# Batch 1's attention issued earlier on TensorE, weight splitting released sooner and paced, and a second PSUM bank for h

## The chip, the cores and the metric

The kernel runs on one core of one Trainium2 chip. Times are device microseconds (us) of one launch; lower is better. Engines are called as the profile calls them: PE is TensorE's matmuls and PEld its weight loads, DVE is VectorE, ACT is ScalarE, POOL is GpSimd, SP is SyncE, whose queue issues every DMA here.

## The reference

```python
def reference(q, k, v, phi, moe_w_in, moe_w_out, moe2_w_in, moe2_w_out):
    # q, k, v: 4 batches x 8 heads x 576 tokens x 64; phi: 4 x 8 x 576 x 32 slots
    a = softmax(phi, axis=2)                     # over the tokens
    k_m, v_m = a^T k, a^T v                      # 32 x 64 per head
    attn = softmax(q k_m^T / 8)                  # 576 x 32 per head
    x = (attn v_m)  -> 2304 tokens x 512
    y = relu(x w_in)^2 w_out                     # 512 -> 2048 -> 512
    h = y w_in2;  g = h tanh(softplus(h))
    return g w_out2                              # 512 -> 2048 -> 512
```

All of it is float32. Each matmul of the two MLPs is done as three products of a high and a low part (high x high, high x low, low x high), so every weight is split into such parts on the chip, too.

## The kernel before

The first MLP is the stage of this change. It works on tiles of half a batch (288 tokens), named by batch and half: `10` is batch 1, half 0. A tile goes through 16 steps `fc`, one for each 128 columns of the hidden layer. A step on PE is six matmuls into one bank (`h10_3` is step 3 of tile 10; L464 to L466), then on ACT a Relu (L472), a Square (L473) and a cast to the high part (L477), on DVE a subtraction that leaves the low part (L480), and three steps later (`LAG`) twelve matmuls of the second weight, `mm2_step`, into four accumulators (L428 to L430; their operand is `g10_3`).

Weights for h are not `w_in` itself: attention's last product (with `v_m`) is folded into it, so `w_part` multiplies the value memory `vT` of a batch with a page of `w_in` (`pw120` is batch 1, page 2; one page serves two steps), and ACT and DVE split the result (`wp`).

Batches 0 and 1 are worked through together, because the first weights arrive while they run: `subs` lists twelve passes, three groups of steps (0 to 3, 4 to 9, 10 to 15) times four tiles (00, 01, 10, 11). In the text, pass 2 is tile 10 of the first group, and so on from pass 0 to pass 11. Batches 2 and 3 follow in passes of 16 steps: pass 12 is tile 20, pass 13 tile 21, passes 14 and 15 batch 3. Then the second MLP runs (lines from L740 on).

Beside the steps run "lanes", small pieces of work that a step takes along: `kv_unit` (softmax of phi, `pt` transposes of it, `pk` products with k and v, `pkt` transposes of the result) and `attn_unit` (scores `psc`, DVE transposes, softmax over 32 slots, a transpose back, and the high and low parts `ah` and `al` that the tile's h needs).

The weights pass through `Conv`: a DMA loads 512 KB (`raw_i1_7`: first MLP's input weight, part 7; `o1` its output weight; `i2`, `o2` those of the second MLP), ACT runs a Prelu on its high words (L190), DVE shifts and merges (L212, L219), and for the output weights ACT casts the high part (L186) and DVE subtracts (L227). `c1` splits the first MLP's 32 parts, `c2` the second's. `c1.limit` bounds how many parts may start, and `c1.after` names an attention unit behind whose DVE work the splitting must stand.

A scheduler sets the order of instructions on each engine from the order of the code and from when it thinks that operands and buffers are free; on the chip each engine then follows that order. PSUM has eight banks: four accumulators, `mm` (h), `b0` (pk and pkt), and a pair `bb` (pt, psc and pw in turn). In before, h has the bank `mm` alone in passes 0 to 12, and takes `mm` and `b0` in turn in pass 13.

## Time and profile before

| | |
|---|---|
| time, median of 3 runs | 819.94 us (819.09 to 820.22) |
| the profiled execution: time, span | 820.21 us, 818.1 us |
| PE busy, of the span | 787.7 us (96%) |
| DVE busy, of the span | 577.1 us (71%) |
| ACT busy, of the span | 459.1 us (56%) |
| TensorE's mean granted clock | 0.979 of full speed |

The span is that of the profiled execution; some 2.1 us of its time lie outside it. A busy time of PE counts overlapping matmuls and modelled ends, so "96% busy" is not 96% of its peak: two matmuls of a step start 0.13 us apart but each is shown as 0.29 us long. Where PE loses time shows better in the distance between starts.

### The profile page before, as it was taken

Reading aid. Unit: us, or ns where it says so; the run is one execution under the profiler, and the core shown is the slowest. Engines: PE = TensorE matmul, PEld = TensorE weight load, DVE = VectorE, ACT = ScalarE, POOL = GpSimd, SP = SyncE. Lnnn points to the kernel's source line nnn. Section 1 sums busy time; section 2 is a strip of 40 time slices with the busy share of each in tenths; the row PEclk is TensorE's granted clock in tenths of the full one; section 3 lists DMA queues with packets and bytes.
Section 4 is the critical chain, followed back from the end, with each engine's and each line's share of the span. In section 5 each row is a group of like instructions: output and inputs, shape, how many; then the busy total and the mean of one; then the engine's idle time right before and its main releaser. Section 6 shows DMA issues by size and latency. Waiting matters only on the chain.

```text
span 818.1 us, 13791 instructions
## 1 busy us (share of the span) xinstructions
PE 787.7 (96%) x5288; PEld 680.7 (83%) x5288; DVE 577.1 (71%) x1023; ACT 459.1 (56%) x916; POOL 119.5 (15%) x104
## 2 busy tenths in 40 slices
PE   5887989999999999999999999999999999999997
PEld 4675877988888998999988888888888888999896
DVE  4958886756876353334478888888878887777774
ACT  3766787756776576434445445544554455555553
POOL 0000000000000000000222134222422142222222
PEclk8697999999999999999999999999999999999999
DMA  8974678977997227604740001100110001001001
GB/s 339 406 272 164 198 261 285 373 284 256 366 344 281 87 95 296 235 2 140 284 150 1 0 1 55 42 1 1 39 52 1 0 20 53 1 1 39 1 2 38
DMA packets 38705, 111.77 MB, mean 137 GB/s; under 512 B 3952, under 2 KB 10096, under 8 KB 38640
## 3 DMA queue, kind: packets, MB, share of 16 engines
q1 hardware_dynamic: 38640, 110.90, 37.5%
q8 instruction: 41, 0.67, 0.3%
q14 instruction: 24, 0.20, 0.1%
HBM read 80.48 MB, written 30.41 MB: 136 GB/s over the span
## 4 chain that ended last, share of the span: by engine, by line
PE 84%; DMA 7%; DVE 5%; ACT 3%; issue 1%; SPq 1%; ACTq 0%; DVEq 0%
PE hb L764 8%; PE hb L763 8%; PE hb L765 8%; PE b L739 8%; PE b L738 8%; PE b L740 8%; PE a L428 7%; PE a L430 7%; PE a L429 7%; DMA raw_i<-in_moe_w_in_dram 6%; PE h L464 4%; PE h L465 3%; PE h L466 3%; PE pw L381 2%; DMA raw_o<-in_moe_w_out_dram 1%; PE pk L295 1%
## 5 line engine op out<-in xcount | busy, mean ns | idle before, releaser
L428 PE MATMUL a<-g,o1h 128*128 128x288 f32 x512 | 150.8, 306 | 3.5 <-ACT g L477 2.6
L429 PE MATMUL a<-g,o1l 128*128 128x288 f32 x512 | 147.2, 298 | 0.0
L791 POOL TENSOR_TENSOR gl<-nh,gh 128x512 fp32r<-128x512 f32 (+1 forms) x80 | 97.6, 1221 | 285.4 <-PE b L740 185.0
L430 PE MATMUL a<-g,o1h 128*128 128x288 f32 x512 | 121.1, 299 | 1.6 <-DVE g L480 1.6
L764 PE MATMUL hb<-yl,i 128*128 128x512 f32 (+1 forms) x320 | 118.8, 371 | 0.0
L763 PE MATMUL hb<-yh,i 128*128 128x512 f32 (+1 forms) x320 | 118.8, 371 | 0.0
L765 PE MATMUL hb<-yh,i 128*128 128x512 f32 (+1 forms) x320 | 118.7, 371 | 0.0
L787 DVE SCALAR_TENSOR_TENSOR n<-n,u 128x512 f32<-128x512 f32 (+1 forms) x80 | 79.6, 995 | 52.5 <-ACT u L783 52.5
L739 PE MATMUL b<-o,gh 128*128 128x512 f32 x288 | 113.5, 394 | 0.0
L738 PE MATMUL b<-o,gh 128*128 128x512 f32 x288 | 113.4, 394 | 0.0
L740 PE MATMUL b<-o,gl 128*128 128x512 f32 x288 | 112.4, 395 | 0.0
L428 PEld LDWEIGHTS a<-g,o1h 128*128 128x128 f32 x512 | 97.4, 191 | 14.2 <-ACT g L477 4.1
L777 ACT ACTIVATE u<-hb 128x512 f32<-128x512 f32 (+1 forms) x80 | 44.4, 555 | 108.1 <-PE hb L765 108.1
L472 ACT ACTIVATE s<-h 128x288 f32<-128x288 f32 x128 | 52.3, 410 | 91.7 <-PE h L466 90.6
L429 PEld LDWEIGHTS a<-g,o1l 128*128 128x128 f32 x512 | 97.9, 191 | 0.0
L430 PEld LDWEIGHTS a<-g,o1h 128*128 128x128 f32 x512 | 86.0, 190 | 6.2 <-issue 2.9
L480 DVE TENSOR_TENSOR g<-s,g 128x288 fp32r<-128x288 f32 x128 | 59.8, 469 | 42.3 <-ACT g L477 41.2
L464 PE MATMUL h<-ah,wp 128*128 128x288 f32 x256 | 80.2, 313 | 6.8 <-ACT s L472 3.6
L714 POOL TENSOR_TENSOR yl<-yr,yh 128x512 fp32r<-128x512 f32 (+1 forms) x16 | 21.3, 1346 | 406.4 <-PE h L466 401.6
L465 PE MATMUL h<-al,wp 128*128 128x288 f32 x256 | 77.4, 302 | 1.7 <-DVE al L371 1.7
L790 ACT CAST gh<-nh 128x512 fp32r<-128x512 f32 (+1 forms) x80 | 46.3, 578 | 57.4 <-DVE nh L789 54.3
L466 PE MATMUL h<-ah,wp 128*128 128x288 f32 x256 | 76.9, 301 | 0.0
(98 smaller groups left out, 1399.4 us busy)
## 6 DMA issues: line engine op xcount, KB each, us to landing
raw_i<-in_moe_w_in_dram SPq DMA_DIRECT2D x32, 512.0 KB, 7.0
raw_o<-in_moe_w_out_dram SPq DMA_DIRECT2D x32, 512.0 KB, 5.9
win1r<-w_i SPq DMA_DIRECT2D x17, 512.0 KB, 5.5
w_i<-st_i SPq DMA_DIRECT2D x16, 512.0 KB, 5.0
w_o<-st_o SPq DMA_DIRECT2D x16, 512.0 KB, 5.1
i<-w_i SPq DMA_DIRECT2D x16, 512.0 KB, 7.5
o<-w_o SPq DMA_DIRECT2D x16, 512.0 KB, 4.1
kv<-in_kvm_dram SPq DMA_DIRECT2D x5, 1024.0 KB, 8.3
```

The costliest lines, as they stand in the source:

```text
L428: nc.tensor.matmul(o, wh[:, c, cs], sh, start=first, stop=False)
L429: nc.tensor.matmul(o, wl[:, c, cs], sh, start=False, stop=False)
L430: nc.tensor.matmul(o, wh[:, c, cs], sl, start=False, stop=last)
L464: nc.tensor.matmul(ph, w[:, 0, hg, fs], hi[:, hg], start=(hg == 0), stop=False)
L465: nc.tensor.matmul(ph, w[:, 0, hg, fs], lo[:, hg], start=False, stop=False)
L466: nc.tensor.matmul(ph, w[:, 1, hg, fs], hi[:, hg], start=False, stop=(hg == 1))
L738: nc.tensor.matmul(acc[t], gh[:, cs], wh, start=(fc == 0), stop=False)
L739: nc.tensor.matmul(acc[t], gh[:, cs], wl, start=False, stop=False)
L740: nc.tensor.matmul(acc[t], gl[:, cs], wh, start=False, stop=(fc == NF - 1))
L763: nc.tensor.matmul(h, wh[:, d * P:d * P + P], yh, start=(d == 0), stop=False)
L764: nc.tensor.matmul(h, wh[:, d * P:d * P + P], yl, start=False, stop=False)
L765: nc.tensor.matmul(h, wl[:, d * P:d * P + P], yh, start=False, stop=(d == 3))
```

## The change

- In pass 0 and pass 1, four steps of tile 01 and one of tile 00 may only be issued on PE behind a piece of batch 1's kv and attention work (`ahead`): `h01_0` behind `pk` of head group 0, `h01_1` behind `pk` of group 1, `h01_2` behind `pkt`, `h01_3` behind the scores `psc10`. `kv_unit(1)` takes both phi softmaxes first, and k and v of one head group go into one bank and one evacuation.
- `c1.limit` grows by three parts (i1_4, i1_5, o1_4) in pass 1, behind attention 01 and no longer behind attention 10.
- From pass 1 on, each Prelu of `c1` must stand behind the Relu of the latest step (`paced`). `c2`'s are not paced.
- In passes 2 to 5 and 7 to 11, h takes `mm` and `b0` in turn. Passes 0, 1, 6 and 12 keep `mm` alone.
- Pass 2 makes no `w_part` of its own; pass 1 does it at its end.

```diff
@@ class Conv
-            self.limit, self.after = len(self.order), None
+            self.limit, self.after, self.paced = len(self.order), None, False
...
-                nc.scalar.activation(high, high, AF.Prelu, scale=2.0 ** -112, alpha=-2.0 ** 32)
+                with behind(marks, "step" if self.paced else None):
+                    nc.scalar.activation(high, high, AF.Prelu, scale=2.0 ** -112, alpha=-2.0 ** 32)
...
+    done_pe = {}
+    ahead = {(0, 0, 3): ("pt", 1, 0), (0, 1, 0): ("pk", 1, 0), (0, 1, 1): ("pk", 1, 1),
+             (0, 1, 2): ("pkt", 1), (0, 1, 3): ("psc", 1, 0)}
@@ kv_unit
-            kv_soft(b, p)
-            yield
+            if b > 1:
+                kv_soft(b, p)
+                yield
             kv_turn(b, p)
             yield
-            if isinstance(kv_t[b, p], tuple):
-                kv_mem(b, p, (0,), tag)
-                kv_mem(b, p, (1,), tag)
-            else:
-                kv_mem(b, p, (0, 1), tag)
+            kv_mem(b, p, (0, 1), tag)
@@ a_tile
+            key = ahead.get((b, half, fc))
             for hg in range(2):
-                nc.tensor.matmul(ph, w[:, 0, hg, fs], hi[:, hg], start=(hg == 0), stop=False)
+                with behind(done_pe, key if hg == 0 else None):
+                    nc.tensor.matmul(ph, w[:, 0, hg, fs], hi[:, hg], start=(hg == 0), stop=False)
...
-            nc.scalar.activation(s, ph, AF.Relu)
+            marks["step"] = nc.scalar.activation(s, ph, AF.Relu)
@@ passes
         if i == 0:
-            lanes = attn_later(0, 1) + kv_later(1) + attn_later(1, 0)
-            n_steps = 2
+            u = lazy(lambda: attn_unit(0, 1, lambda: load_q(1, 1)))
+            lanes = [[u, 1], [soft_both(1), 1], [u, 3]] + kv_later(1) + attn_later(1, 0)
+            n_steps = 3
         elif i == 1:
             assert (0, 1) in a_t
-            n_steps = 3
+            c1.limit, c1.after, c1.paced = 2 * GROUPS[0] + 3, (0, 1), True
+            n_steps = 1
         elif i == 2:
             drain(lanes)
             c1.limit, c1.after = len(c1.order), (1, 0)
-            lanes, n_steps = attn_later(1, 1), 1
+            lanes, n_steps = [[iter(range(1)), 1]] + attn_later(1, 1), 1
...
-            if fc % 2 == half == 0 and fc + 2 < f1:
+            if fc % 2 == half == 0 and fc + 2 < f1 and i != 2:
                 c1.need("i1", fc + 3)
                 w_part(b, fc // 2 + 1, 0, 256)
+            if i == 1 and fc + 1 == f1:
+                w_part(1, fc // 2, 0, 256)
...
-        a_tile(b, half, f0, f1, tick, mid, post)
+        a_tile(b, half, f0, f1, tick, mid, post, ("mm",) if i in (0, 1, 6) else ("mm", "b0"))
```

What this does to the order of instructions, at three places.

PE, from the middle of pass 1 to the first step of pass 2, before (mm2's rows are left out):

```order
L307 MATMUL pkt10_621<-ident_96,kk1_524 128x128 x2
...
L464 MATMUL h01_3_739<-ah01_442,wp01_413 128x288
...
L340 MATMUL psc10_653<-q100_231,kT1_624 32x288 x4
...
L381 MATMUL pw100_727<-win1_0_288,vT1_626 32x256 x8
...
L340 MATMUL psc11_782<-q110_377,kT1_624 32x288 x4
...
L464 MATMUL h10_0_768<-ah10_705,wp10_736 128x288
L381 MATMUL pw110_808<-win1_1_392,vT1_626 32x256 x8
L465 MATMUL h10_0_768<-al10_706,wp10_736 128x288
```

And of the change:

```order
L315 MATMUL pkt10_588<-ident_96,kk1_506 128x128 x2
...
L345 MATMUL psc10_595<-q100_231,kT1_591 32x288 x4
...
L471 MATMUL h01_2_701<-ah01_450,wp01_421 128x288
...
L386 MATMUL pw100_738<-win1_0_288,vT1_593 32x256 x8
L471 MATMUL h01_3_750<-ah01_450,wp01_421 128x288
...
L386 MATMUL pw110_780<-win1_1_400,vT1_593 32x256 x8
...
L471 MATMUL h10_0_796<-ah10_685,wp10_747 128x288
L471 MATMUL h10_1_826<-ah10_685,wp10_747 128x288
...
L345 MATMUL psc11_845<-q110_377,kT1_591 32x288 x4
```

The scores of tile 10 moved ahead of steps 2 and 3 of pass 1, and the scores of tile 11 from ahead of tile 10's first step to behind its second. Between psc10 and h10_0 stand 24 matmuls of mm2 and pw100 in before; of the change 36 of mm2, 12 of h, pw100 and pw110.

DVE, from the end of attention 11's softmax to its low part `al11`, of before:

```order
L363 STREAM_TRANSPOSE at11_914<-x11_791 128x576
L212 TENSOR_SCALAR win1_3_947<-raw_i1_6_362 128x4x128
L227 TENSOR_TENSOR o1l2_944<-ct_o1_4_903,o1h2_943 128x512
...
L254 TENSOR_REDUCE mx20_2357<-phi0_79 128x1
L254 TENSOR_REDUCE mx21_2473<-phi1_81 128x1
L219 SCALAR_TENSOR_TENSOR win1_3_947<-raw_i1_6_362,win1_3_947 128x4x128
L371 TENSOR_TENSOR al11_917<-at11_914,ah11_916 128x576
L212 TENSOR_SCALAR ct_o1_6_1060<-raw_o1_6_427 128x512
L480 TENSOR_TENSOR g10_1_836<-s10_1_835,g10_1_836 128x288
```

And of the change:

```order
L368 STREAM_TRANSPOSE at11_946<-x11_854 128x576
L214 TENSOR_SCALAR ct_o1_6_965<-raw_o1_6_435 128x512
L229 TENSOR_TENSOR o1l2_804<-ct_o1_5_918,o1h2_803 128x512
...
L260 TENSOR_REDUCE mx20_2355<-phi0_79 128x1
L260 TENSOR_REDUCE mx21_2471<-phi1_81 128x1
L393 TENSOR_TENSOR wp03_1150<-pw030_1141,wp03_1150 128x512
L221 SCALAR_TENSOR_TENSOR ct_o1_6_965<-raw_o1_6_435,ct_o1_6_965 128x512
L452 COPY ys100_1046<-a1001_793 128x288
L376 TENSOR_TENSOR al11_949<-at11_946,ah11_948 128x576
```

Ten instructions stand between `at11` and `al11` in both. In before g10_1 to g10_3 come behind al11; of the change all four of pass 2's low parts stand ahead of at11.

PE, where batch 2's `pk200` stands. In before, in pass 6 (tile 10, steps 4 to 9), in pieces:

```order
L381 MATMUL pw160_2383<-win1_6_1514,vT1_626 32x256 x8
L295 MATMUL pk200_2417<-kv20_617,et20_2363 32x128 x7
L428 MATMUL a1040_1502<-g10_4_1520,o1h2_943 128x288
...
L464 MATMUL h10_6_1576<-ah10_705,wp13_1544 128x288
...
L295 MATMUL pk200_2417<-kv20_617,et20_2363 32x128 x7
L430 MATMUL a1040_1502<-g10_4_1520,o1h2_943 128x288
```

And of the change, in pass 10 (tile 10, steps 10 to 15), in one piece:

```order
L471 MATMUL h10_12_2453<-ah10_685,wp16_2390 128x288
...
L303 MATMUL pk200_2415<-kv20_562,et20_2361 32x128 x16
L303 MATMUL pk200_2415<-kt2_564,et20_2361 32x128 x4
L473 MATMUL h10_12_2453<-ah10_685,wp16_2390 128x288
...
L386 MATMUL pw170_2493<-win1_7_1661,vT1_593 32x256 x8
```

The four products pk200, pk210, pk300 and pk310 are in 19 pieces in before and whole in the change; batch 2's moved from passes 6 and 7 to pass 10. (The trace counts each of these fp32 matmuls twice.)

## Rows read from the trace of the kernel before

**Rows 1.** Busy time in stretches: length, PE, PEld, DVE, ACT, POOL, PEclk, DMA share, GB/s.

```profile
56.37:78.19 21.82, 13.22 (x105) 9.39 (x97) 19.13 (x40) 11.87 (x28) 0.00 (x0) 0.77 0.32 100
78.19:96.11 17.92, 17.92 (x160) 15.63 (x160) 16.79 (x38) 13.43 (x30) 0.00 (x0) 1.00 0.61 202
96.11:150.00 53.89, 48.82 (x431) 41.12 (x429) 41.60 (x85) 41.81 (x91) 0.00 (x0) 0.97 0.80 279
...
245.60:287.80 42.20, 42.20 (x358) 39.33 (x357) 21.23 (x44) 25.63 (x58) 0.00 (x0) 1.00 0.47 177
287.80:330.60 42.80, 42.80 (x407) 38.15 (x405) 20.23 (x39) 27.30 (x64) 0.00 (x0) 1.00 0.51 187
```

**Rows 2.** PE in order of time, passes 1 to 2: start, us, instruction, idle before.

```profile
58.70 0.72 PE L340 MATMUL psc<-q,kT 64*32 64x288 f32 x16 [1.54 <-issue]
61.34 0.61 PE L464 MATMUL h<-ah,wp 128*128 128x288 f32 x1 [1.93 <-ACT ah L370]
```

**Rows 3.** DVE in order of time, 53 to 78 us, attention 10 and 11.

```profile
53.13 0.85 DVE L349 STREAM_TRANSPOSE x<-psc 128x288 f32<-128x288 f32 x2 [1.16 <-PE psc L340]
...
61.48 0.84 DVE L349 STREAM_TRANSPOSE x<-psc 128x288 f32<-128x288 f32 x2
...
63.41 0.75 DVE L371 TENSOR_TENSOR al<-at,ah 128x576 fp32r<-128x576 f32 x1
...
69.06 0.75 DVE L357 TENSOR_REDUCE ssm<-x 128x18 f32<-128x576 f32 x1 [2.37 <-ACT x L354]
...
71.81 0.78 DVE L363 STREAM_TRANSPOSE at<-x 128x576 f32<-128x576 f32 x1
...
76.68 0.75 DVE L371 TENSOR_TENSOR al<-at,ah 128x576 fp32r<-128x576 f32 x1
```

**Rows 4.** Who waited for whom, 96 to 150 us: total, times, longest.

```profile
ACT raw_i L190 <- DMA raw_i<-in_moe_w_in_dram: 9.8, 10, 3.0
PEld a L428 <- ACT g L477: 3.6, 4, 1.4
...
PEld h L464 <- ACT s L472: 2.8, 3, 1.2
```

**Rows 5.** PE in order of time: pk whole and cut, pw, and the step's beat.

```profile
38.78 1.08 PE L295 MATMUL pk<-kv,et 128*32 128x128 f32 x32
...
40.02 0.77 PE L273 MATMUL pt<-ident,phi 128*128 128x128 f32 x5
...
135.69 0.66 PE L381 MATMUL pw<-win,vT 64*32 64x256 f32 x16
136.29 0.64 PE L295 MATMUL pk<-kv,et 128*32 128x128 f32 x14
136.85 0.40 PE L428 MATMUL a<-g,o1h 128*128 128x288 f32 x1
...
148.28 0.41 PE L295 MATMUL pk<-kt,et 128*32 128x128 f32 x2
148.62 0.40 PE L464 MATMUL h<-ah,wp 128*128 128x288 f32 x1
...
275.35 0.69 PE L430 MATMUL a<-g,o1h 128*128 128x288 f32 x4
...
277.74 0.69 PE L430 MATMUL a<-g,o1h 128*128 128x288 f32 x4
```

**Rows 6.** Loads of kv (1 MB), 100 to 260 us: issue to landing.

```profile
DMA to landing us min/median/max: 4.9/8.1/8.3
```

**Rows 7.** DVE in order of time, pass 12: a weight part's three operations and a low part.

```profile
247.59 0.69 DVE L227 TENSOR_TENSOR st_o<-ct_o,st_o 128x512 fp32r<-128x512 f32 x1 [1.12 <-ACT st_o L186]
248.32 0.43 DVE L212 TENSOR_SCALAR ct_o<-raw_o 128x512 int32<-128x512 int32 x1
248.66 0.45 DVE L480 TENSOR_TENSOR g<-s,g 128x288 fp32r<-128x288 f32 x1
...
250.49 0.68 DVE L219 SCALAR_TENSOR_TENSOR ct_o<-raw_o,ct_o 128x512 int32<-128x512 int32 x1
```

More of the change, by code (lines that the diff above doesn't have):

```diff
@@ L139, in behind @@
     @contextlib.contextmanager
-    def behind(key):
+    def behind(table, key):
         if key is None:
@@ L145, in behind @@
         else:
-            with tc.issue_after(marks[key].ins):
+            with tc.issue_after(table[key].ins):
                 yield
@@ L189, in tick @@
                 high = self.raw[key, u][:, :, 1].bitcast(F32)
-                nc.scalar.activation(high, high, AF.Prelu, scale=2.0 ** -112, alpha=-2.0 ** 32)
+                with behind(marks, "step" if self.paced else None):
+                    nc.scalar.activation(high, high, AF.Prelu, scale=2.0 ** -112, alpha=-2.0 ** 32)
                 self.started += 1
                 self.flight.append([key, u, 0, None, None])
-            with behind(self.after):
+            with behind(marks, self.after):
                 self.fields(bits, ends, between)
@@ L252, in kv_soft @@
         mx = Y.tile([P, 1], F32, tag="mx", name=f"mx{b}{p}", bufs=2)
-        with behind((1, 1) if b == 2 else None):
+        with behind(marks, (1, 1) if b == 2 else None):
             nc.vector.tensor_reduce(out=mx, in_=ph, op=ALU.max, axis=AX.X, negate=True)
@@ L272, in kv_turn @@
         for i in range(NC + 1):
-            nc.tensor.transpose(
+            done_pe["pt", b, p] = nc.tensor.transpose(
                 outs[i // 4][:, (i % 4) * P:(i % 4) * P + P], phi_t[p][:, i * P:i * P + P], ident)
@@ L285, in kv_mem @@
         ps = bank(tag, f"pk{b}{p}{lo}").rearrange("p (s d) -> p s d", d=D)
-        for c in range(NC + 1):
-            blk = c if p == 0 else (c + 1) % (NC + 1)
-            for g in range(4):
-                if c == NC:
-                    src = kt_t[b][:, lo:hi, g]
-                elif len(which) == 2:
-                    src = kv_t[b, p][:, :, g, c]
-                else:
-                    src = kv_t[b, p][lo][:, g, c]
-                nc.tensor.matmul(
-                    ps[M * g:M * g + M, lo:hi], et_t[p][:, blk, M * g:M * g + M], src,
-                    start=(c == 0), stop=(c == NC))
+        both = not isinstance(kv_t[b, p], tuple)
+        for a, z in [(lo, hi)] if both else [(i, i + 1) for i in which]:
+            for c in range(NC + 1):
+                blk = c if p == 0 else (c + 1) % (NC + 1)
+                for g in range(4):
+                    if c == NC:
+                        src = kt_t[b][:, a:z, g]
+                    elif both:
+                        src = kv_t[b, p][:, a:z, g, c]
+                    else:
+                        src = kv_t[b, p][a][:, g, c]
+                    done_pe["pk", b, p] = nc.tensor.matmul(
+                        ps[M * g:M * g + M, a:z], et_t[p][:, blk, M * g:M * g + M], src,
+                        start=(c == 0), stop=(c == NC))
         if (b, "k") not in kk_t:
@@ L306, in kv_heads @@
         for i in which:
-            nc.tensor.transpose(
+            done_pe["pkt", b] = nc.tensor.transpose(
                 ps[:, i * P:i * P + P], kk_t[b, "k"][:, i].rearrange("p a d -> p (a d)"), ident)
@@ L317, in kv_unit @@
         for p in range(2):
-            kv_soft(b, p)
-            yield
+            if b > 1:
+                kv_soft(b, p)
+                yield
             kv_turn(b, p)
             yield
-            if isinstance(kv_t[b, p], tuple):
-                kv_mem(b, p, (0,), tag)
-                kv_mem(b, p, (1,), tag)
-            else:
-                kv_mem(b, p, (0, 1), tag)
+            kv_mem(b, p, (0, 1), tag)
             nxt(p)
@@ L339, in attn_unit @@
             for p in range(2):
-                nc.tensor.matmul(
+                done_pe["psc", b, half] = nc.tensor.matmul(
                     ps[M * g:M * g + M, p, :T], kT[b][D * p:D * p + D, M * g:M * g + M],
@@ L543, in lazy, with soft_both @@
         yield from f()
+    def soft_both(b):
+        kv_soft(b, 0)
+        kv_soft(b, 1)
+        yield
     def kv_later(b):
@@ L554, in kv_later @@
         u = lazy(lambda: kv_unit(b, "b0", nxt))
-        return [[u, 3], [iter(range(2)), 2], [u, 4]] if b > 1 else [[u, 7]]
+        return [[u, 3], [iter(range(2)), 2], [u, 4]] if b > 1 else [[u, 5]]
     def attn_later(b, half):
```

## The prediction

> **What bounds the kernel now.** I read first the busy times by stretch [rows 1], because a mean over the span hides that only one part loses time. From 245.6 us on PE is busy for the whole of each stretch at the full granted clock, and there a step of 18 matmuls takes the 2.39 us between two ends of mm2 [rows 5], or 0.133 us a matmul. With that beat I can say what PE loses in the early stretches. From 56.37 to 78.19 us the order has 48 matmuls of steps, two pw and one psc; at 0.133 us, and 0.6 us for a pw [rows 5] and as much for psc, that is 8.2 us of work in 21.8 us, at a mean granted clock of 0.77 [rows 1]: 13.6 us are lost. From 96.11 to 150 us there are 431 matmuls [rows 1], of which the order makes 112 pw (7 x 0.6 us), 5 pt (0.5 us) and 40 pk (2.2 us in its pieces), so 274 of steps: 43.3 us of work in 53.9 us, 10.6 us lost. Between these two, PE is busy throughout. So some 24 us of the 818 are open to a change of order here, and everything else is PE's own work.
>
> Who is waited for differs. In the first stretch PE idles before psc11 and then for `ah10` [rows 2]: attention 10 begins on DVE at 53.13 and its low part ends at 64.16 us [rows 3], while PE has run out of pass 1. DVE is busy 19.1 of the 21.8 us there [rows 1], and attention 11, begun at 61.48, has its low part only at 77.43 us [rows 3]. In the second stretch ACT is held ten times by a weight load, 9.8 us in all, and PEld waits 3.6 us for ACT's casts and 2.8 us for its Relu [rows 4]: a Prelu that waits for its DMA has Relus and casts queued behind it.
>
> **The change part by part.** I make the sum against the profiled execution's own 820.2 us (0.3 above the median).
>
> *Attention 10 earlier.* Before psc10 the change leaves out two h (12 matmuls) and 16 of mm2, 3.7 us, and adds a wait of about 0.5 us for ACT, which has to empty two accumulators ahead of h01_1's Relu. So attention 10 starts on DVE 3.2 us sooner than its 53.13 [rows 3], at about 49.9. By the order DVE then has some 8.2 us of work up to the end of al10, plus about 1 us for the exponential on ACT: al10 at 59 us. PE fills this time with 48 matmuls and two pw (7.5 us) and waits about a microsecond. psc11 follows at 60.2 us behind two steps of tile 10, and its transposes start on DVE at about 61.5, as in before.
>
> *Attention 11 is late next.* Between its transposes and the end of al11, DVE has by the order 24 instructions: the attention's own eight, four low parts g10, one merge of a weight, one evacuation of a pw, and the ten between at11 and al11. DVE's instructions follow each other some 0.08 us sooner than their lengths say (0.43 at 248.32, the next at 248.66 [rows 7]), so a shift counts 0.34, a low part 0.37, 512 columns 0.6 and 576 columns 0.67 us [rows 3, 7]: 12.8 us with the transposes. About 2 us of waits for ACT's casts and its exponential come on top, and al11 ends near 76.3, a microsecond before its 77.43 [rows 3]. PE is through with pass 2 and pw030 by 70.3 and waits there for six microseconds, since h11_0's second matmul and all that follows stand behind it. But it then has behind it what before still had to do at 78.19: 28 matmuls and pw030, 4.3 us. Progress at 76.3 equals that of before at 82.5: a gain of 6 us (3 to 8, if ACT's waits are 3 us longer, or none).
>
> *The clock.* The first stretch's mean of 0.77 means 10 us at the lower level, 1.2 GHz, after the idle time before psc11 and h10_0. The new wait of six microseconds is longer than either idle there, so I expect a spell of low clock behind it, and now with work waiting for PE. Its cost lies between nothing and 5 us (10 us at half speed, all of it PE's); I take 2.5.
>
> *Passes 4 to 7.* Pacing puts the Prelus of i1_12 and after behind h01_8 on ACT instead of among h00_4 to h00_9, and by then their loads have long landed, so a Relu no longer stands behind a Prelu that waits. Two banks add that h's next step need not wait for the last Relu. I count as won the 9.8 us of stalls as far as PE felt them, two thirds of the 10.6 us: 7 (3 to 9, since casts are still in ACT's queue behind a Prelu of 0.7 us, and the second MLP's splits are not paced).
>
> Here a rule of the Trainium skill speaks against a part of the change: the page "TensorE: Matmul & The Clock Gate" (section "HAM oscillation — how this bites in real kernels") reports that adding PSUM double-buffering to a matmul kernel whose loop was in good order brought no further gain. The trace has 2.8 us of waits for Relu [rows 4] that a second bank could take; by the rule none of it would be won and the forecast would be 3 us higher.
>
> *pk whole.* A whole pk takes 1.24 us (38.78 to 40.02), but 14 of its 40 matmuls cut out take 0.56 and two of them 0.34 [rows 5]. The four pk that are cut today into 19 pieces add up to 8.3 us; whole they are 5.0. Against this pw is cut once more than before (0.5 us), and fewer returns to steps save about as much. Gain 3.3 us (2 to 5).
>
> *What comes in its place.* With h in b0, batch 2's pk can't slip in early; it comes in pass 10 and in a row. pk210 needs a kv load that is issued when pk200 is through; 9.6 us of PE's work lie between, and such loads took 4.9 to 8.3 us [rows 6], so it is hidden by a little. psc20 stands directly behind pkt20 and needs ACT's copy of it, and h10_15 needs that bank back: about 1.5 us. And the second MLP's splits slide: ten more parts of o2 fall into pass 12, at 1.8 us of DVE each [rows 7], and attention 21 and three pw with them. DVE's 21.2 us of 42.2 there [rows 1] grow to about 45 of 46. Where DVE was as full (16.8 of 17.9 us) [rows 1], PE lost under a microsecond; I take 2 for pass 12. Together -3.5 us (-1 to -8).
>
> *Sum:* 6 - 2.5 + 7 + 3.3 - 3.5 = 10.3 us, so 809.9 us for the profiled execution, and against the median **809.5 us**.
>
> **The rivals.** (a) *The stall only moves.* Since al11 ends no sooner than today, DVE stays the bound up to pass 4; the low clock costs its full 5 us, and the second stretch wins 4 of its 10.6 us, because the Prelus that it loses come back in passes 6 to 9. 6 - 5 + 4 + 3.3 - 3.5 = 4.8: 815.2 us. For it: DVE's 88% in that stretch. Against: DVE has the three early parts behind it and the conversion is not needed before pass 4.
>
> (b) *All of it is won.* The low clock doesn't come back, passes 10 to 12 hide their work: 6 + 9 + 4 - 1 = 18, 802 us. For it: no wait of PE in those passes today.
>
> (c) *Slower: DVE in pass 12.* Each of the ten parts that slide there stands in DVE's queue ahead of a low part that PE needs. If each held PE for its whole 1.8 us, 18 us would be lost where I counted 2: 809.5 + 16 = 825.5. It decides, that is, ends above 821.5, once PE pays for about eight of the ten. Against it: mm2 runs three steps, 7 us, behind its h, and DVE's list is no longer than the pass.
>
> (d) *The clock under alternating banks.* In pass 13 h already takes two banks in turn, and the granted clock is 1.00 [rows 1]. The same page of the Trainium skill (section "A second HAM failure mode: psum-queue depth-cycling") tells of a kernel whose PE, cycling through PSUM banks, idled briefly and often enough for its clock to go back and forth; the trace bears none of it out. If the nine passes (50 steps of 2.39 us) did a quarter of their work at half speed, 30 us would be lost, 839.5 us.
>
> (e) *No change:* gains and new waits cancel, 819 to 821 us.
>
> **How the numbers follow.** Chances: the forecast 52%, (a) 24%, (b) 11%, (c) 6%, (d) 1%, (e) 6%. The forecast's own range, from the bounds of its terms taken half together, is 804 to 815. The range that leaves out no more than 2 in 10 reaches from (b) to beyond (a): 801 to 818 us. A measurement of this kernel tells about 0.2%, 1.6 us, from no change. Faster by more: the forecast, (b) and nearly all of (a), 86%; the same: (e) and an edge of (a), 6%; slower 8%.
>
> **What would show it.** Right, if PE's idle time before h10_0 shrinks to about a microsecond and one wait of 4 to 7 us stands before the second matmul of h11_0, for al11; if the chip begins pass 4 (h00_4) 5 to 9 us sooner; if ACT's waits for loads between passes 4 and 7 fall below 4 us; if a pk takes 1.2 us in one piece; if PE shows waits of 1 to 2 us around psc20. Wrong, if al11 comes later than 78 us, if low clock lasts over 10 us behind it, if pk210 waits for its kv, or if PE has gaps at every step of pass 12.

## The result, and the profile after

The changed kernel takes 809.73 us (median of 4 runs, 808.44 to 810.99) against 819.52 us for the kernel before in the same session: a ratio of 0.9878, 95% interval 0.9858 to 0.9897. The profiled execution took 809.73 us, 10.5 us less than the profiled one of before; its span is 807.9 us, 10.2 us less.

Busy time in stretches (length; PE, PEld, DVE, ACT, POOL, each with its count; PEclk; DMA share; GB/s), to be read beside [rows 1]:

```profile
56.99:70.96 13.97, 13.05 (x126) 10.70 (x124) 12.50 (x26) 9.95 (x25) 0.00 (x0) 1.00 0.41 160
70.96:83.16 12.20, 7.97 (x52) 7.16 (x53) 11.03 (x26) 8.63 (x22) 0.00 (x0) 0.72 0.16 51
83.16:150.00 66.84, 66.84 (x537) 59.27 (x536) 40.38 (x85) 45.63 (x107) 0.00 (x0) 1.00 0.46 154
150.00:221.50 71.50, 69.28 (x638) 63.46 (x636) 47.18 (x101) 48.83 (x115) 0.00 (x0) 1.00 0.86 305
221.50:277.50 56.00, 50.06 (x513) 44.05 (x514) 45.11 (x92) 38.17 (x85) 0.00 (x0) 1.00 0.92 341
277.50:320.30 42.80, 42.80 (x406) 38.16 (x405) 25.23 (x48) 29.92 (x70) 0.00 (x0) 1.00 0.77 287
...
73.40:80.30 6.90, 4.58 (x19) 4.58 (x20) 6.21 (x17) 4.63 (x13) 0.00 (x0) 0.51 0.07 29
```

Pass 2 (the first line) is now worked through; pass 3 (the second) idles, and the last line shows why its clock is 0.72 of full speed: in these 6.9 us the mean is 0.51, so some 6.8 of them are at the lower level, 1.2 GHz. Passes 4 to 7 (the third) have PE busy throughout, with DMA at 0.46, and passes 8 to 11 (the fourth) nearly so, with DMA at 0.86. The loss has moved to pass 12 (the fifth): PE busy 50.06 of 56.00 us, with DMA at 0.92, where before it was busy throughout with DMA at 0.47. This pass has 513 matmuls where before's had 358: work of batches 2 and 3 that slid into it (five more pw, one more pk and one more psc).

PE in order of time, the same kernel, with the scores of attentions 10 and 11, the start of pass 3, and batch 2's kv in pass 10 [rows 2, 5]:

```profile
48.29 0.72 PE L345 MATMUL psc<-q,kT 64*32 64x288 f32 x16
...
60.16 0.72 PE L345 MATMUL psc<-q,kT 64*32 64x288 f32 x16
...
70.96 0.53 PE L471 MATMUL h<-ah,wp 128*128 128x288 f32 x2 [0.37 <-ACT ah L375]
75.72 0.61 PE L472 MATMUL h<-al,wp 128*128 128x288 f32 x1 [4.23 <-DVE al L376]
...
200.25 1.08 PE L303 MATMUL pk<-kv,et 128*32 128x128 f32 x32
201.15 0.40 PE L303 MATMUL pk<-kt,et 128*32 128x128 f32 x8
...
204.98 0.72 PE L345 MATMUL psc<-q,kT 64*32 64x288 f32 x16 [0.37 <-ACT kT L319]
```

The stalls ahead of psc11 and `h10_0` are gone, and one wait of 4.2 us for `al11` has come, at the place and of the kind that the prediction named. pk210 (200.25) waits for nothing and is whole.

Who waited for whom on ACT in passes 4 to 7 (first line, total, times, longest), and ACT and PE from 217 to 278 us:

```profile
ACT raw_i L192 <- DMA raw_i<-in_moe_w_in_dram: 1.4, 1, 1.4
...
ACT raw_o L192 <- DMA raw_o<-in_moe_w_out_dram: 5.4, 3, 2.8
ACT st_o L187 <- DMA w_o<-st_o: 4.5, 2, 3.8
...
ACT st_i L187 <- DMA win1r<-w_i: 3.0, 1, 3.0
ACT st_o L187 <- DMA w_i<-st_i: 2.7, 1, 2.7
...
PE h L471 <- ACT s L479: 2.2, 1, 2.2
PE a L433 <- ACT g L484: 1.5, 1, 1.5
```

In passes 4 to 7 ACT waits once for a raw weight where it waited ten times [rows 4]. But six of those ten waits, 6.0 of 9.8 us, were the second MLP's, whose Prelus the change does not pace. In before its parts come from 118 us on, as DVE's first shift of one shows (its output is `ct_i`, that of the first MLP's `win`); the second line is ACT's waits from 117 to 150 us:

```profile
118.96 0.42 DVE L212 TENSOR_SCALAR ct_i<-raw_i 128x512 int32<-128x512 int32 x1
...
ACT raw_i L190 <- DMA raw_i<-in_moe_w_in_dram: 6.0, 6, 3.0
```

In the changed kernel no Prelu of the first MLP waits any more from 83 us on, and the second MLP's have moved: they wait 16.8 us in all from 83 to 278 us, where in before they waited 10.0 us. Around pass 12 it waits 15.6 us for DMA, in two ways: a Prelu for its raw weight, and a cast for a buffer of the staging ring (`st_i`, `st_o` and the reloaded pages `win1r` share four buffers), which a write or a reload still holds. PE waits for ACT's Relu and cast, not for DVE. ACT in order of time shows how a DMA gets there:

```profile
227.24 0.67 ACT L192 ACTIVATE raw_o<-raw_o 128x512 f32<-128x512 f32 x1 [2.79 <-DMA raw_o<-in_moe_w_out_dram]
227.80 0.42 ACT L484 CAST g<-s 128x288 fp32r<-128x288 f32 x1
...
229.12 0.41 ACT L479 ACTIVATE s<-h 128x288 f32<-128x288 f32 x1
232.20 0.62 ACT L187 CAST st_o<-ct_o 128x512 fp32r<-128x512 f32 x1 [2.67 <-DMA w_i<-st_i]
```

The Prelu waits 2.79 us for its load, and the cast of g, which mm2 needs, stands behind it; the next wait, for the ring, comes five microseconds later.

### The profile page after: what moved, and what is told of

It is laid out like the page before. It is cut to its first block, busy times and chain, and to the rows that moved or that the text cites. A ratio compares the mean times of both kernels' runs of the same rounds, so it can differ in the third digit from the quotient of the medians.

```text
span 807.9 us, 13777 instructions
## 1 busy us (share of the span) xinstructions
PE 776.5 (96%) x5288; PEld 676.5 (84%) x5288; DVE 577.8 (72%) x1022; ACT 452.3 (56%) x916; POOL 119.4 (15%) x104
## 4 chain that ended last, share of the span: by engine, by line
PE 80%; DMA 8%; DVE 7%; ACT 3%; issue 1%; SPq 0%; ACTq 0%; DVEq 0%
PE hb L781 8%; PE hb L780 8%; PE hb L782 8%; PE b L756 8%; PE b L755 8%; PE b L757 8%; PE a L433 6%; PE a L435 6%; PE a L434 6%; DMA raw_i<-in_moe_w_in_dram 3%; PE h L471 3%; PE h L472 3%; PE h L473 3%; DMA w_i<-st_i 2%; PE pw L386 1%
## 5 line engine op out<-in xcount | busy, mean ns | idle before, releaser
L433 PE MATMUL a<-g,o1h 128*128 128x288 f32 x512 | 150.3, 301 | 3.0 <-ACT g L484 1.5
L434 PE MATMUL a<-g,o1l 128*128 128x288 f32 x512 | 149.2, 297 | 0.0
L435 PE MATMUL a<-g,o1h 128*128 128x288 f32 x512 | 134.8, 295 | 0.7 <-DVE g L487 0.7
L433 PEld LDWEIGHTS a<-g,o1h 128*128 128x128 f32 x512 | 96.5, 189 | 11.1 <-ACT g L484 4.0
L435 PEld LDWEIGHTS a<-g,o1h 128*128 128x128 f32 x512 | 90.7, 188 | 3.0 <-DVE g L487 1.6
L807 ACT CAST gh<-nh 128x512 fp32r<-128x512 f32 (+1 forms) x80 | 46.3, 579 | 57.4 <-DVE nh L806 54.3
```

The costliest lines, as they stand in the source:

```text
L433: nc.tensor.matmul(o, wh[:, c, cs], sh, start=first, stop=False)
L434: nc.tensor.matmul(o, wl[:, c, cs], sh, start=False, stop=False)
L435: nc.tensor.matmul(o, wh[:, c, cs], sl, start=False, stop=last)
```

## The experiments

Twelve other kernels, each timed in five rounds beside the kernel before on the same chip. The kernel before took 820.5 to 820.9 us there, so ratios to it are compared, not microseconds: one part in a thousand is 0.8 us. The first four columns of times are the starts of passes in the profiled execution (the first matmul of their first h), which show where a kernel wins or loses; pass 0 began at 21.8 to 23.8 us in them, so a microsecond or two in a start need not be the kernel's own. The two columns behind them are estimates of what PE lost on steps in passes 4 to 7 and in pass 12: the time from the start of each step matmul to that of the next matmul, less 0.133 us [rows 5], summed.

| kernel | pass 4 | pass 8 | pass 12 | pass 13 | lost, 4 to 7 | lost, 12 | median us | ratio to before (95%) |
|---|---|---|---|---|---|---|---|---|
| before | 91.5 | 172.6 | 245.6 | 287.8 | 11.2 | 1.3 | | 1 |
| changed | 83.2 | 150.4 | 221.5 | 277.5 | 2.5 | 8.7 | 809.7 | 0.9878 (0.9858 to 0.9897) |
| one bank | 86.8 | 166.1 | 238.0 | 283.8 | 9.0 | 2.6 | 816.5 | 0.9955 (0.9939 to 0.9970) |
| not paced | 81.4 | 151.6 | 222.8 | 277.5 | 7.0 | 7.5 | 813.1 | 0.9909 (0.9884 to 0.9933) |
| old hand-out | 81.5 | 150.7 | 221.8 | 276.2 | 2.7 | 7.1 | 809.7 | 0.9870 (0.9852 to 0.9888) |
| late release | 83.8 | 150.8 | 223.2 | 278.4 | 3.6 | 7.0 | 809.5 | 0.9869 (0.9850 to 0.9888) |
| the bank alone | 85.7 | 156.8 | 228.7 | 286.0 | 4.7 | 8.6 | 819.1 | 0.9983 (0.9971 to 0.9995) |
| three undone | 84.6 | 156.3 | 228.6 | 282.7 | 7.5 | 6.7 | 815.4 | 0.9941 (0.9922 to 0.9961) |
| pw back | 82.1 | 149.4 | 222.6 | 278.1 | 2.5 | 7.4 | 811.7 | 0.9891 (0.9868 to 0.9914) |
| c2 paced | 83.9 | 150.2 | 224.8 | 275.1 | 2.0 | 2.9 | 808.3 | 0.9850 (0.9834 to 0.9866) |
| fewer splits | 83.0 | 150.4 | 222.6 | 277.9 | 2.6 | 7.5 | 812.5 | 0.9906 (0.9889 to 0.9923) |
| al11 first | 76.3 | 144.2 | 216.3 | 270.6 | 3.0 | 7.1 | 804.1 | 0.9803 (0.9783 to 0.9823) |
| al11 first, c2 paced | 76.2 | 143.3 | 218.6 | 268.7 | 2.8 | 2.7 | 802.8 | 0.9783 (0.9765 to 0.9802) |
| al11 first, c2 paced late | 76.1 | 144.0 | 217.0 | 270.5 | 3.0 | 6.7 | 803.3 | 0.9785 (0.9767 to 0.9802) |

**One bank.**

```diff
-        a_tile(..., ("mm",) if i in (0, 1, 6) else ("mm", "b0"))
+        a_tile(..., ("mm",))
```

> The changed kernel with h in one bank in all of the first batches' passes; the attention order, the early release and the pacing stay. By the order batch 2's pk goes back among the steps of passes 6 to 11, in pieces, and pass 12 has that much less to do. By the prediction's terms the second bank is worth 3.3 us in the pk that are whole and up to 2.8 us in waits for Relu, and it costs most of the 8 us that PE loses in pass 12 of the changed kernel: 811 to 814 us, with ACT's waits for DMA in passes 4 to 7 still below 4 us. Rival A, the second bank carries the 10 us that passes 4 to 7 won: their time goes back up by 5 us or more, 815 to 819 us. Rival B, the second bank wins nothing beside the whole pk, as the Trainium skill's page TensorE: Matmul & The Clock Gate (HAM oscillation) reports of another kernel, while pass 12 gets its 8 us back: 803 to 807 us.

Measured 0.9955: rival A. Without the second bank 0.0077 of the time comes back, 6.3 us, and passes 4 to 7 (the first line) take 12 us longer. In them ACT waits 5.1 us for raw weights, a little above the 4 us expected, and none of it for the first MLP's paced ones; PE still loses 9.0 us on steps, where before lost 11.2. Of the 6.3 us the pk are 4.1: they are in 21 pieces again and take 9.0 us. Pass 12 (the second line) does lose less, as expected: it has 410 matmuls, PE is busy throughout, and ACT waits there for no DMA.

```profile
86.80:166.10 79.30, 74.13 (x606) 62.27 (x604) 48.52 (x102) 52.02 (x118) 0.00 (x0) 1.00 0.55 176
...
238.00:283.80 45.80, 45.80 (x410) 40.11 (x407) 31.68 (x65) 32.17 (x71) 0.00 (x0) 1.00 0.88 323
```

**Not paced.**

```diff
-            c1.limit, c1.after, c1.paced = 2 * GROUPS[0] + 3, (0, 1), True
+            c1.limit, c1.after, c1.paced = 2 * GROUPS[0] + 3, (0, 1), False
```

> The changed kernel without the pacing of ACT's Prelus; banks, order and release stay. If the pacing carries what passes 4 to 7 won, ACT is held by weight loads again (before: ten times, 9.8 us; in the changed kernel once, 1.4 us), and 4 to 8 us of the 10 come back: 814 to 818 us. Rival, the second bank alone covers those stalls, because PE can be a step further ahead of ACT: ACT's waits come back in the trace, PE's do not, and the time is 808 to 811 us.

Unclear in time: 0.9909, its interval overlapping that of the changed kernel, with runs from 809.9 to 816.3 us. The median, 813.1 us, lies between the two expectations, and the trace is that of the fastest execution. In it ACT's waits for loads from 83 to 150 us come back in full (first two lines), and a part of them reaches PE, which loses 7.0 us on steps in passes 4 to 7 and not 2.5 (third line, the largest of its waits, 81 to 152 us):

```profile
ACT raw_i L192 <- DMA raw_i<-in_moe_w_in_dram: 10.6, 8, 3.1
ACT raw_o L192 <- DMA raw_o<-in_moe_w_out_dram: 5.5, 5, 1.6
...
PE h L471 <- ACT s L479: 3.5, 5, 1.2
```

From pass 4 to pass 8 it takes 70.2 us, 3.0 more than the changed kernel, but it entered pass 4 1.8 us sooner, and at pass 13 the two profiled executions are level. With two banks, pacing by itself is worth between nothing and 5 us; neither theory is shown.

**Old hand-out.** The lanes and steps of passes 0 to 2 as before, and no `ahead`; k and v of one head group stay in one accumulator. `ahead` was not undone by itself, nor was the one accumulator.

```diff
-            lanes = [[u, 1], [soft_both(1), 1], [u, 3]] + kv_later(1) + attn_later(1, 0)
-            n_steps = 3
+            lanes = attn_later(0, 1) + kv_later(1) + attn_later(1, 0)
+            n_steps = 2
...
-            lanes, n_steps = [[iter(range(1)), 1]] + attn_later(1, 1), 1
+            lanes, n_steps = attn_later(1, 1), 1
```

> The changed kernel with the work of batch 1's kv and attention handed out among the steps of passes 0 to 2 as before the change (so the order of PE has psc10 and psc11 behind as many h and mm2 as before); banks, release and pacing stay. By the prediction attention 10 earlier is worth 6 us, less 2.5 of low clock: 813 to 815 us, psc10 3 to 4 us later than the 48.29 us of the changed kernel and the low part of attention 11 at 78 us or later. Rival, the end of attention 11 is set by DVE's list of weight parts and comes at 76 to 77 us all the same, since DVE does these parts while it would wait for psc10: pass 4 begins within 1.5 us of the changed kernel's 83.2 us, 809 to 811 us.

Measured 0.9870, the rival. PE in order of time:

```profile
49.50 0.71 PE L345 MATMUL psc<-q,kT 64*32 64x288 f32 x16
...
62.41 1.21 PE L345 MATMUL psc<-q,kT 64*32 64x288 f32 x16
...
76.12 0.41 PE L472 MATMUL h<-al,wp 128*128 128x288 f32 x1 [2.22 <-DVE al L376]
```

psc10 comes at 49.50, only 1.2 us later than in the changed kernel, since pk110 is taken in one go here too. psc11 is later by 2.2 us, but `al11` ends at 76.1 us, only 0.4 us later than in the changed kernel. DVE does nearly the same list of work up to there (125 instructions against 128) in another order, and PE arrives later and waits less.

**Late release.**

```diff
-            c1.limit, c1.after, c1.paced = 2 * GROUPS[0] + 3, (0, 1), True
+            c1.paced = True
```

> The changed kernel without the sooner release: in pass 1 the conversion stops after eight parts as before, so the parts i1_4, i1_5 and o1_4 are split in pass 2 and not in pass 1; the rest stays. If DVE is the bound up to pass 4 and has idle time in pass 1, the three parts, with 1.8 us of DVE each, come back in front of pass 4: 812 to 815 us, and pass 4 begins 2 to 5 us later than 83.2 us. Rival, those parts stand in front of attention 10 on DVE today, and without them attention 10 and then attention 11 end a microsecond or two sooner while the weights are still in time for pass 4: 806 to 809 us.

Measured 0.9869, between the two expectations: neither. The wait for `al11` is 4.3 us and ends at 75.1 us, pass 4 begins 0.6 us later, and nothing of it is left at the end that can be told.

**The bank alone**, on the kernel before.

```diff
-        a_tile(b, half, f0, f1, tick, mid, post)
+        a_tile(b, half, f0, f1, tick, mid, post, ("mm",) if i in (0, 1, 6) else ("mm", "b0"))
```

> The kernel before with one part of the change alone: h takes two banks in turn in the same passes as in the changed kernel; order of the attention, release and pacing as before. If the second bank is what carries the early stretch too (with the old hand-out of the attention's work the time stayed 0.9870 of before, without the sooner release 0.9869), most of the gain is here: 811 to 814 us against a before of 820 us, pass 4 begins at 82 to 86 us and not at 91.5, and pk is whole. Rival, the parts add up as the prediction has it: the bank alone is worth its pk (3.3 us) and the 6 us of passes 4 to 7 that it lost when it was taken out, less the waits of pass 12, 815 to 818 us, and pass 4 begins at 90 us or later.

Measured 0.9983: less than both expectations. Pass 4 does begin 5.8 us sooner, and at pass 12 this kernel is 16.9 us ahead of before. But ahead of pass 4 it has done 36 step matmuls (of 276) and one pw less, 5.4 us of work put off, so the bank wins almost nothing there. What it wins is in passes 4 to 7, 6.5 us on steps, and in pass 12 it runs into the same loss as the changed kernel (DMA 0.91), so that at pass 13 it is 1.8 us ahead:

```profile
228.70:286.00 57.30, 51.58 (x513) 44.83 (x513) 45.20 (x92) 38.31 (x85) 0.00 (x0) 0.97 0.91 335
```

**Three undone**: old hand-out, late release and no pacing together; the second bank and the place of the pw stay. The edits are those of the second, third and fourth experiment.

> The changed kernel with three of its parts undone at once: the hand-out of the attention's work as before, no sooner release, no pacing. What stays is the second bank, the two halves of batch 1's second pk in one accumulator, and the pw of batch 1 and of weight pair 2 at their new places. Undone one at a time the three parts cost nothing, nothing and 0.3%; the bank alone gave 0.2%. If they stand in for one another, so that one of the three is needed, the time goes up here by 4 us or more, 814 to 818 us. Rival, none of the three matters and what works together with the second bank is the place of the pw (and the one accumulator): 809.5 to 812.5 us, pass 4 begins by 84 us.

Measured 0.9941, within the first expectation. Undone one at a time the three parts cost nothing that can be told (0.9909, 0.9870, 0.9869 against 0.9878, intervals overlapping); together they cost 0.0063, 5.2 us. That they stand in for one another is likely but not shown: the three single costs add up to 0.0014, and the 0.0049 that is missing has an uncertainty as large. In the trace most of the cost, 4.5 us, lies in passes 4 to 7, and there the run without pacing loses 3.0 us by itself. Ahead of pass 4 the picture is that of parts standing in: with any one undone PE ends the stretch waiting 2.2 to 4.3 us for `al11`; with all three it waits sooner (2.1 us for `ah10`, 1.2 for `al10`, 2.0 for a low part of g) and no longer for `al11`, which ends at 78.3 us, or 76.9 if the later start of this execution is taken off.

**The pw back.**

```diff
-            if fc % 2 == half == 0 and fc + 2 < f1 and i != 2:
+            if fc % 2 == half == 0 and fc + 2 < f1:
...
-            if i == 1 and fc + 1 == f1:
-                w_part(1, fc // 2, 0, 256)
```

> The changed kernel with the pw back at their old places: pw110 and pw020 behind the first steps of pass 2, not pw110 at the end of pass 1; all else stays. A pw takes the accumulator pair that the scores of attention 11 use. In the kernel before PE waited 1.3 and 1.5 us ahead of these two pw, and with the bank alone 1.3 and 0.6 us. If their place is what makes the second bank useful, these waits come back, attention 11 or pass 2 is later, pass 4 begins at 86 us or later and the time is 812 to 816 us. Rival, as with the order of the attention: attention 11's end is set by DVE's list, PE waits for it anyway, and the time stays at 809 to 811 us.

Measured 0.9891, not to be told from the changed kernel: the rival. The waits ahead of the pw don't come back (pw110 and pw020 take 0.59 us each, their length without a wait), pass 3 begins at 70.2 us, and PE waits 4.2 us for `al11` as before this edit. (In the trace of before PE idles 0.5 and 0.3 us ahead of these two pw, less than the expectation says.)

**The second MLP's splits paced.**

```diff
-              lambda i: (Y, "raw", 3))
+              lambda i: (Y, "raw", 3)); c2.paced = True
```

> The changed kernel with the second MLP's Prelus paced as the first's are: each stands on ACT behind the latest step's Relu. In pass 12 of the changed kernel PE loses about 8 us, and ACT waits 5.4 us for raw weights and 10.2 us for buffers of the staging ring. If ACT, held in its order, is the cause, at least the first of these falls below 2 us and the time to 805 to 808 us. Rival A, DMA is the bound there (0.92 busy, 341 GB/s): the parts slide, the waits stay, 809 to 811 us. Rival B, as the prediction has it, DVE is full in pass 12: the waits of ACT go and PE waits for DVE, 809 to 811 us.

Measured 0.9850, 808.3 us, at the edge of the first expectation; the interval still touches that of the changed kernel. From 217 to 278 us ACT waits 0.2 us for raw weights (5.4 before this edit). Pass 12 takes 50.3 us instead of 56.0, with 80 instructions on DVE there instead of 92, as some splits slid past it; PE loses 2.9 us on steps in it and not 8.7, with DMA even busier:

```profile
224.80:275.10 50.30, 49.44 (x503) 44.30 (x503) 39.78 (x80) 35.79 (x79) 0.00 (x0) 1.00 0.96 349
```

About 4 us are given back in pass 10, where ACT in order of time reads:

```profile
207.20 0.62 ACT L187 CAST st_i<-ct_i 128x512 fp32r<-128x512 f32 x1 [7.21 <-DMA w_i<-st_i]
207.73 0.27 ACT L319 ACTIVATE kT<-pkt 128x128 f32<-128x128 f32 x1
```

A cast waits 7.2 us for a buffer of the ring, and the copy `kT` that psc20 needs stands behind it.

**Fewer splits in pass 12.**

```diff
-        c2.tick(start=fc % 3 != 2)
+        c2.tick(start=fc % 2 == 0)
```

> The changed kernel with the second MLP's splits started in every second step of passes 12 and 13 and not in two of three. If the DMA traffic of these splits holds ACT in pass 12 (15.6 us of waits, DMA 0.92 busy), the waits halve, PE's 8 us there fall to 3 to 5, and the parts that slide into pass 13 are hidden, since PE waits for nothing there: 805 to 807 us. Rival, the waits at the head of pass 12 come from what was started in passes 8 to 11 and stay: 808 to 811 us. A second rival: the last splits slide past pass 13 and the second MLP begins later, 811 us or more.

Measured 0.9906: no faster. DMA in pass 12 stays at 0.92 and 336 GB/s, ACT's waits for DMA are 16.1 us, and PE loses 7.5 us on steps there where it lost 8.7. In its trace, that of the fastest execution, this is the first rival. The second isn't seen there: the second MLP's first matmul comes 0.5 us later, and pass 13 began as much later. The median, 812.5 us, is in the second rival's range; what the other executions lose no trace shows.

**Attention 11's low part first.**

```diff
-        nc.vector.tensor_sub(lo, a, hi.bitcast(F32))
+        marks["al11" if (b, half) != (1, 1) else (1, 1)] = nc.vector.tensor_sub(lo, a, hi.bitcast(F32))
```

The splitting and batch 2's maxima, which had to stand behind `at11`, now stand behind `al11`.

> The changed kernel with attention 11's low part taken ahead, on DVE, of eight instructions (parts of the conversion and batch 2's two maxima) that stand between its last transpose and it. By their rows these take 3.8 us, so the low part ends near 72 us, PE's wait of 4.5 us before the second matmul of h11_0 shrinks to a microsecond, and the spell of low clock behind it goes. If the prediction's first term is right in kind, the time falls by 3 to 5 us, to 805 to 807 us. Rival, from the run with the old hand-out (pass 4 began 1.7 us sooner and pass 8 at the same time): what PE gains ahead of pass 4 is waited for again in pass 4, where the weights' conversion on DVE is the bound; pass 4 begins near 80 us, pass 8 at 150 us, and the time stays at 809 to 811 us.

Measured 0.9803, 0.0075 or 6.2 us better than the changed kernel: the first theory, and more than it asked. DVE in order of time, first of the changed kernel:

```profile
69.43 0.78 DVE L368 STREAM_TRANSPOSE at<-x 128x576 f32<-128x576 f32 x1
70.13 0.38 DVE L214 TENSOR_SCALAR ct_o<-raw_o 128x512 int32<-128x512 int32 x1
70.43 0.68 DVE L229 TENSOR_TENSOR o1l<-ct_o,o1h 128x512 fp32r<-128x512 f32 x1
71.03 1.09 DVE L214 TENSOR_SCALAR win<-raw_i 128x512 int32<-128x512 int32 x3
72.04 1.41 DVE L260 TENSOR_REDUCE mx<-phi 128x1 f32<-128x576 f32 x2
73.36 0.68 DVE L393 TENSOR_TENSOR wp<-pw,wp 128x512 fp32r<-128x512 f32 x1
73.96 0.68 DVE L221 SCALAR_TENSOR_TENSOR ct_o<-raw_o,ct_o 128x512 int32<-128x512 int32 x1
74.56 0.45 DVE L452 COPY ys<-a 128x288 f32<-128x288 f32 x1
74.92 0.75 DVE L376 TENSOR_TENSOR al<-at,ah 128x576 fp32r<-128x576 f32 x1
```

and of this one:

```profile
69.22 0.78 DVE L368 STREAM_TRANSPOSE at<-x 128x576 f32<-128x576 f32 x1
69.92 0.65 DVE L393 TENSOR_TENSOR wp<-pw,wp 128x512 fp32r<-128x512 f32 x1
70.49 0.44 DVE L452 COPY ys<-a 128x288 f32<-128x288 f32 x1
70.86 0.74 DVE L376 TENSOR_TENSOR al<-at,ah 128x576 fp32r<-128x576 f32 x1
```

`al11` comes 4.1 us sooner, because the ten instructions ahead of it are two. PE waits 0.4 us for it. With the wait the spell of low clock is gone: the granted clock is 1.00 from 40 to 143 us,

```profile
40.00:143.00 103.00, 101.22 (x933) 88.92 (x933) 76.68 (x162) 75.07 (x178) 0.00 (x0) 1.00 0.56 192
```

and pass 4 begins 6.9 us sooner: 4 us of wait, some 2 us of matmuls that no longer run at half speed, and 1 us of work that comes later (four step matmuls and a pw). The rival falls: from pass 4 to pass 8 this kernel takes 67.9 us against 67.2, so almost nothing is waited for again.

**Both together**: al11 first, and c2 paced from its start.

> Two of the experiments in one kernel: attention 11's low part ahead of eight instructions on DVE, and the second MLP's Prelus paced. If their gains are apart (0.0075 in the first stretch, about 0.0028 in pass 12), the ratio to before is 0.976 to 0.978, 800.5 to 802.5 us against a before of 820.5. Rival, pass 12 is bound by DMA (0.92 busy), so an earlier start only runs into the same transfers: the ratio stays at the 0.9803 of the first alone, 804 us.

Measured 0.9783, near the first expectation, but its interval and that of al11 first overlap: the second gain is not shown. Pass 12 takes 50.1 us instead of 54.3, and ACT's casts for `st_i` wait 16.1 us for the ring from 143 to 270 us. One of these waits, 7.7 us in pass 10, holds the copy `kT` again: PE waits 3.2 us for it, and the granted clock is at the lower level from 200.5 to 207.3 us.

**al11 first, and c2 paced from pass 12 on.**

```diff
-    b, nb = 2, 3
+    b, nb, c2.paced = 2, 3, True
```

> Attention 11's low part ahead of eight instructions on DVE, as in the fastest runs so far, and the second MLP's Prelus paced from pass 12 on only. Paced from the start, ACT had a cast waiting 7.2 us for a buffer of the staging ring in pass 10, with the copy of kT that psc20 needs queued behind it, which gave back some 4 us of what pass 12 won. If pass 12's loss is ACT held in its order by the raw loads, PE's gaps there fall from 6.7 us (with the low part alone) to 2 to 3, nothing is lost in pass 10, and the ratio is 0.973 to 0.977, 798.5 to 801.5 us. Rival, DMA is the bound in pass 12 (0.94 to 0.96 busy), and what was won with pacing came from parts that had slid out of pass 12: the ratio stays at 0.979 to 0.981, 803 to 805 us.

Measured 0.9785, closer to the rival. ACT's waits from 216 to 271 us with al11 first alone:

```profile
ACT raw_o L192 <- DMA raw_o<-in_moe_w_out_dram: 6.6, 2, 4.0
...
ACT st_o L187 <- DMA w_i<-st_i: 2.7, 2, 2.1
ACT st_o L187 <- DMA w_o<-st_o: 2.2, 3, 1.8
```

and with late pacing too:

```profile
ACT st_o L187 <- DMA w_i<-st_i: 5.2, 2, 3.7
```

The waits for raw weights are gone, but those for the ring stay, and pass 12 takes 53.5 us instead of 54.3, with 6.7 us lost on steps, not the 2 to 3 expected. Taking one of two kinds of waits out of ACT's order wins nothing here that can be told.

## Why the prediction was right, and where its terms were not

The forecast of 809.5 us was met (809.7), but its terms were off in both directions, and two of its reasons did not hold, so that the number came out this near is partly luck. What PE lost on steps is the estimate of the table above. (By its own terms the sum is 809.6 against the median, and (c) and (d) together are 7%, where 8% is given for slower; neither matters.)

- **What bounds the kernel: right.** The two stretches that the prediction called open to a change were where the time was won, and passes 13 to 15 and the second MLP kept their length: the lead at pass 13 is 10.3 us, that of the spans 10.2.
- **Attention 10 and 11, +6, and the clock, -2.5: the size right, the reason only in part.** The chain came as foretold: psc10 at 48.29, attention 10 on DVE at 49.5 (49.9 foretold), psc11 at 60.16 (60.2), the end of `al11` at 75.7 (76.3); PE's wait for it was 4.2 us (six foretold), and the low clock lasted 6.8 us and cost about 2.2. Pass 4 begins 8.3 us sooner (5 to 9 foretold), of which 3.2 are 24 step matmuls that come later now; 5.2 us are won in this stretch, net of the clock, where 3.5 was foretold. The second bank has almost no part in them: alone it wins 0.4 us here, and everything but the bank begins pass 4 4.7 us sooner with no work put off. But the prediction gave this to the work left out ahead of psc10, and with the old hand-out nothing is lost. With the old hand-out, with one bank and with the bank alone PE ends the stretch waiting for `al11` as in the changed kernel (2.2, 2.9 and 2.3 us). DVE's list up to it was named in the prediction as what is late next; that cutting it is worth 6 us, the run with al11 first shows. Not tested by itself is k and v in one accumulator, which every kernel but the bank alone has.
- **Passes 4 to 7, +7: 8.7 measured, but not by the means foretold.** PE lost 11.2 us on steps there before and 2.5 after. The prediction counted "the 9.8 us of stalls as far as PE felt them" as won by pacing, with the bank to add to it. Of these 9.8 us 6.0 were the second MLP's, which are not paced (the prediction has that only as a reason for its lower bound); they left these passes because its splits start later, and so the sign "below 4 us" came true (1.4 us). And the paced ones gone, PE loses nearly as much with one bank: 9.0 us. With the bank alone it loses 4.7, although ACT waits 12.8 us for raw weights there. So the bank carries most of this term; pacing and the other parts add to it, pacing by itself with an uncertainty as large as its 0.0031. Whether the bank wins by the Relu that PE need not wait for, or by the pk that it keeps out of these passes, the runs do not tell apart.
- **The Trainium skill's report on double-buffered PSUM** ("TensorE: Matmul & The Clock Gate", section "HAM oscillation — how this bites in real kernels": no further gain in a loop in good order). By it the forecast would have been 3 us higher. The bank alone seems to agree with it (1.4 us), but its trace does not: 6.5 us are won on steps in passes 4 to 7, and 7.3 lost in pass 12 to work that slid there. Beside the other parts, taking the bank out costs 6.3 us, of which the pk in pieces are 4.1; here the measurement goes against the report.
- **pk whole, +3.3: 3.4 measured.** The four pk take 1.23 us each, 4.9 in all, against 8.3. The pw, which the prediction had at no gain, took 1.1 us less from pass 4 on.
- **What comes in its place, -3.5: about -8, the term that was mis-sized.** psc20's part was small: 0.6 us around pkt20 and 0.4 in h10_15; pk210 was hidden. Pass 12 lost 7.5 us more on steps than before's, where 2 was foretold. The step that failed is "DVE's 21.2 us of 42.2 there [rows 1] grow to about 45 of 46", with DVE as the only bound considered. DVE did grow to 45.1 us, but the pass to 56.0, by the 7.5 us and 6.3 of PE's own work that slid in. What held PE was ACT: all five of PE's waits there, 1.0 to 2.2 us each, name it, and it waits in its order for the second MLP's DMAs, whose Prelus and casts the change had not paced. Before's pass 12 has no such wait (DMA 0.47 [rows 1]), but passes 8 to 11, from which this work slid, had 6.5 us of them; the prediction counted the splits' DVE time and not what they make ACT wait for. With the terms as measured, 5.2 + 8.7 + 3.4 + 1.1 - 8 is 10.4, the lead of 10.3.
- **The rivals.** (a) and (b) did not happen. (c) had the place right and the mechanism wrong, and PE has five waits in pass 12, not one at every step. (d): in the changed kernel the granted clock is 1.00 from pass 4 to pass 13, so the cycling that the Trainium skill's page ("TensorE: Matmul & The Clock Gate", section "A second HAM failure mode: psum-queue depth-cycling") tells of isn't there. (e) did not happen.

The loss of pass 12 is not wholly settled. Shown is that pacing the second MLP's splits from their start takes away ACT's waits for raw weights, and 5.8 of the 8.7 us that PE loses on steps in pass 12 (4.4 of 7.1 with al11 first), and that waits for the staging ring come in their place in pass 10. A share of DMA's time near 1 is not enough to hold PE. In pass 11 of before it was 0.98, at 353 GB/s, with PE busy throughout:

```profile
228.90:245.60 16.70, 16.70 (x141) 14.81 (x140) 13.70 (x28) 13.29 (x31) 0.00 (x0) 1.00 0.98 353
```

So whether pass 12 is DMA-bound in the sense of the Trainium skill's page "Perfetto Trace Analysis" (section "What "DMA-bound" means", first case: the 16 DMA engines themselves) is not shown; in the kernels here it has 0.88 to 0.96 of DMA's time and 320 to 354 GB/s. A rival was left untested: pass 12 keeps one bank for h. In passes 8 to 11 of the changed kernel, with two, ACT waits 15.8 us for DMA (12.6 in pass 12 itself), and PE loses no more on steps than in before (4.1 against 4.3 us). Whether a second bank in pass 12, a larger ring or fewer bytes would free it was not tried.

Three kernels beat both: al11 first (0.9803), with c2 paced (0.9783), and with c2 paced late (0.9785), 802.8 to 804.1 us. They can't be told apart, and the first is one line away from the changed kernel.

## What to carry to other kernels

Undo each part of a change and also do it alone, and ask what work is done by the time a stage begins, not only when it begins: here the bank alone began pass 4 5.8 us sooner, and 5.4 of that was work put off. Before a wait is counted as won, look whose wait it is: six of ten here belonged to work that the change did not touch. When PE waits for one instruction of another engine, read that engine's rows backwards from it: moving one subtraction ahead of eight others gave more than half as much as the whole change. And work in the background that an earlier stage no longer does has to fit where it lands, by what its engine must wait for as well as by its engine time.

## What the runs showed of the hardware

- A single idle time of 4.2 us on PE was followed by the lower clock, with matmuls starting 0.24 us apart instead of 0.13. It set in at 73.4 us, within the wait, which ended at 75.7, and lasted 6.8 us. With a wait of 0.4 us at that place the clock stayed at the upper level (al11 first).
- In other kernels the same wait was shorter: 2.2 us with no low clock behind it (old hand-out), and 2.3, 2.9 and 3.0 us with 3.4 us of it, which set in 0.8 to 1.0 us after the wait's end (the bank alone, one bank, not paced).
- Two banks for h in turn, with no wait of PE in 66.8 us, ran at a granted clock of 1.00.
- DMA's 16 engines were busy 0.98 of 16.7 us at 353 GB/s while PE was busy throughout (before, pass 11).
